# Block kernel: the Q/K stacks as blocks of 16 rows, with a second tile of tokens 768 to 2047

## The chip, the cores and the metric

The kernel runs on one core of a Trainium2 chip. A core has a matrix engine (TensorE, "PE" in the profile, with "PEld" for the loading of its weights), a vector engine (DVE), a scalar engine (ACT), GpSimd (POOL) and a sync engine (SP), from which this kernel issues its DMA transfers. The engines run their own instruction streams and meet at semaphores. Sixteen DMA engines carry the transfers. The metric is the device time of one execution in microseconds (us).

## What is computed

A transformer block for one sequence of 2048 tokens of width 640: attention with 32 heads of 20 dimensions, in which a token sees itself and the 255 tokens before it, and then a gated MLP with a mixing over the tokens. Cut to the part that the change touches:

```python
qkv = (layernorm(x) @ wqkv).reshape(B, S, 3, H, Dh).transpose(2, 0, 3, 1, 4)   # S 2048, H 32, Dh 20
q, k, v = qkv[0], qkv[1], qkv[2]
scores = einsum("bhqd,bhkd->bhqk", q, k) * Dh ** -0.5
mask = (idx[:, None] - idx[None, :] >= 0) & (idx[:, None] - idx[None, :] < 256)
p = softmax(where(mask, scores, -1e9), axis=-1)
h = x + einsum("bhqk,bhkd->bhqd", p, v).reshape(B, S, D) @ wo
h2 = h + gated_mlp(layernorm(h))
```

## The kernel before

**Stages.** By the profile's time: layer norm and V from 0 to 75 us, the projections to Q and K from 75 to 240 ("dense stage"), attention from about 240 to 468, the output projection to 550, then the MLP. The change touches the second and third stage.

**Splitting in three.** Q and K in float32 are each split in three bfloat16 parts (0 the largest). `split_qk(m, c)` does that for one of ten row tiles m (0 to 4 for the first 16 heads, 5 to 9 for the others; the 128 rows of a tile are eight of the 2 x 20 dimensions of Q and K, times 16 heads) and one of four column pieces c (512 tokens each), and stores all three parts with one DMA (L619) to `qk_d` in DRAM, 40 in all.

**Stacks.** Heads are worked in eight groups g of four. For a group, `load_stack(g)` reads Q and K back as stacks: a product of two numbers split in three is formed by laying six pairs of parts, (0,0), (0,1), (0,2), (1,0), (1,1), (2,0), one below another, so that a single matmul over 6 x 20 = 120 rows gives the sum of six products. `a` is 0 for Q and 1 for K. The stack of a group is in two tiles b, of 1024 tokens each (float32 words hold two bfloat16). Each load (L329) takes one part of one `a` and one b: 20 rows of 8 KB (four heads by 512 words) into partitions j, j+6, j+12 ... (`st[b][j:6 * DH:6, a]`), so 24 loads of 160 KB a group. Three sets of tiles are used in turn (`slot0`, `slot1`, and `xb`, which is the third set): group g takes set g mod 3.

**Items.** `max_item(g, qb, hh)` finds the row maxima of 128 queries of one head: four matmuls (L359), each of 32 queries against 288 keys, at four places of one bank, and a reduction on DVE (L369). For the first items it is one matmul of up to 384 keys (L363). `max_rows(g, b)` turns the maxima of eight blocks into three rows, stores them to `m_d` (L384) and loads them as rows 120 to 122 of the stack (L386). `score_item(u, hh)` then computes 128 keys against up to 384 queries over 123 rows, again in four strips (L412), and ACT takes the exponential (L415); `pv_item` multiplies with V and stores the output (L462).

**Cut strips.** Strips of keys or queries that cross token 1024 are in two tiles. `tokens()` (L332) yields the one or two pieces of a strip, and a matmul is issued for each piece, with its own weight load.

**Order.** PE, DVE, ACT and SP run in the order in which the program is written. The attention is a loop over steps s (L760), 16 to a group: in a step stand four max items of block s + 18 and four score items of block s in turns, and pieces of `pv_item(s - 2)`. `load_stack` is a generator; every `next` issues one DMA. In the dense stage three are drawn at a time; in the attention loop `1 + s % 2` in a step (24 in 16 steps). So loads for group s // 16 + 2 stand on SP's queue between the output stores and row loads of the steps. A DMA of SP also waits for the one issued eight before it.

Of the kernel before, what the change touches and what calls it, by code (L numbers as in the profile page):

```python
# [15 lines left out]
P = 128  # L16
S = 2048
# [17 lines left out]
def block_kernel(ctx, tc, x, xt, wqk, wv, wo, w_in, wsp, bsp, w_out, out):  # L35
# [15 lines left out]

    qk_d = dram.tile([2, 3, 2, 2 * DH, H // 2, S // 4], F32, name="qk_d")
    m_d = dram.tile([8, 2, 3, 32, 64], F32, name="m_d")
# [202 lines left out]
    with ExitStack() as ab:  # L256
# [8 lines left out]
        s0 = pool(low0, "slot0p")  # L265
        s0 = [s0.tile([P, 2 * S], F32R, name=f"slot0_{i}") for i in range(2)]
        xn = [h.rearrange("p (a k t) -> p a k t", a=2, k=KD) for h in (xa[:, :CH], xa[:, CH:], *xb)]
# [10 lines left out]
        add_slot(0, s0)  # L278
        add_slot(2, [h[:, :2 * S] for h in xb])
        mask = tmp2.tile([P, 384], BF16, name="mask")  # L280
# [35 lines left out]
        def load_stack(g):  # L316


            st = slot_w[g % 3]
            if g < 3:  # L320
                for h in st:
                    nc.gpsimd.memset(h[96:P, 1], ONES)
                    if g == 2:
                        yield
            for b in range(2):
                for j, parts in enumerate(((0, 0), (0, 1), (0, 2), (1, 0), (1, 1), (2, 0))):
                    for a in range(2):
                        src = qk_d[g // 4, parts[a], b, a * DH:(a + 1) * DH, g % 4 * 4:g % 4 * 4 + 4]
                        nc.sync.dma_start(st[b][j:6 * DH:6, a], src)  # L329
                        yield  # L330

        def tokens(st, rows, a, hh, t0, n):  # L332

            o = 0
            while o < n:
                c, t = divmod(t0 + o, S // 2)
                w = min(n - o, S // 2 - t)
                yield o, w, st[c][:rows, a, hh, t:t + w]
                o += w

        def one(st, rows, a, hh, t0, n):
            (_, _, x), = tokens(st, rows, a, hh, t0, n)
            return x

        def max_item(g, qb, hh, strips=True):

            st = slot_ap[g % 3]
            ps = s1_tile()
            lo = max(0, qb - 2) * P
            n = (qb + 1) * P - lo  # L350
            keep = mask[:, 384 - n:]
            if strips:
                skip = 32 if qb > 1 else 0
                if skip:
                    n, keep = 288, strip
                for j in range(4):
                    q0 = qb * P + 32 * j
                    for o, w, k in tokens(st, 120, 1, hh, lo + skip * j, n):
                        nc.tensor.matmul(ps[32 * j:32 * j + 32, o:o + w], one(st, 120, 0, hh, q0, 32), k,  # L359
                                         start=True, stop=True, tile_position=(0, 32 * j))  # L360
            else:
                for o, w, k in tokens(st, 120, 1, hh, lo, n):
                    nc.tensor.matmul(ps[:, o:o + w], one(st, 120, 0, hh, qb * P, P), k, start=True, stop=True)  # L363
            b, c = divmod(qb, 8)
            if c == 0 and hh == 0:
                m_cols[g, b] = tmp2.tile([P, 32], F32, tag="mcol", bufs=2, name=f"mcol{g}_{b}")
            junk = tmp2.tile([P, 384], BF16, tag="junk", bufs=2, name=f"junk{g}_{qb}_{hh}")
            c += hh * 8
            nc.vector.tensor_tensor_reduce(out=junk[:, :n], in0=ps[:, :n], in1=keep, scale=1.0,  # L369
                                           scalar=NEG, op0=OP.add, op1=OP.max, accum_out=m_cols[g, b][:, c:c + 1])  # L370

        def max_rows(g, b):

            ps = s1_tile()[:32, :P]
            nc.tensor.matmul(ps, m_cols.pop((g, b)), ident, start=True, stop=True)
# [10 lines left out]
            nc.sync.dma_start(slot_w[g % 3][b][120:123, 0], rows.rearrange("a (h r) c -> a h (r c)", h=4))  # L386
            yield
# [3 lines left out]
        def score_item(u, hh):  # L391
# [14 lines left out]
            for i in range(4):  # L406
                k0 = kb * P + 32 * i
                b, e = 32 * i, min(n, 32 * i + 288)
                if NU - NT < u and 4 * (u - NU + NT - 1) + hh < 6:
                    b, e = 0, n  # L410
                for o, w, q in tokens(st, 123, 0, hh, kb * P + b, e - b):
                    nc.tensor.matmul(ps[32 * i:32 * i + 32, b + o:b + o + w], one(st, 123, 1, hh, k0, 32), q,  # L412
                                     start=True, stop=True, tile_position=(0, 32 * i))
            if u <= NU - NT:
# [50 lines left out]
        if True:  # L465
# [137 lines left out]
            def split_qk(m, c, ps):  # L603
# [13 lines left out]
                T = S // 4  # L617
                base = qk_d[m // 5, 0, c // 2, m % 5 * 8, 0, c % 2 * 256:c % 2 * 256 + 256]
                nc.sync.dma_start(bass.AP(tensor=base.tensor, offset=base.offset,  # L619
                                          ap=[[T, P], [2 * 2 * DH * H // 2 * T, 3], [1, 256]]), sg.bitcast(F32))  # L620

# [84 lines left out]
            for n in range(24):  # L706
# [11 lines left out]
                if n >= 20:  # L718
                    for _ in range(3):
                        next(ld0, None)  # L720
            def dense_tail():
                split_wqk(8)
                split_wqk(9)
                for n, (m, c) in enumerate((m, c) for c in range(4) for m in (6, 7, 8, 9)):
# [3 lines left out]
                    if n == 7:  # L728
                        x01.close()
                        s1 = pool(x01, "slot1p", side="right")  # L730
                        add_slot(1, [s1.tile([P, 2 * S], F32R, name=f"slot1_{i}") for i in range(2)])
                    if n >= 7:
                        for _ in range(3):
                            next(ld1, None)

            dense = dense_tail()
            for n in range(12):
                next(dense, None)
                if n % 5 == 4:
                    for _ in range(3):  # L740
                        next(ld0, None)
            for u in range(LEAD):
# [8 lines left out]
                if u in (9, 17):  # L751
                    next(rows)
            assert next(dense, 0) == 0 and next(ld0, 0) == 0
            for _ in after[0]:
# [5 lines left out]
        for s in range(NU + 2):  # L760
            if s % NT == 0 and s < 6 * NT:
                ld = load_stack(s // NT + 2)
            for _ in range(1 + s % 2 if s >= NT else 2 * min(s, 1)):
                next(ld, None)
# [798 lines left out]
```

## Time and profile before

| what | value |
|---|---|
| median of 3 runs | 1105.15 us (1104.84 to 1106.06) |
| profiled execution, its own time | 1106.78 us |
| span of the profiled execution | 1105.1 us |
| PE busy over the span | 97%, 11059 matmuls recorded |
| DVE, ACT, POOL busy | 71%, 55%, 28% |
| granted TensorE clock | 1.00 |
| stack loads L329 | 192 of 160 KB, 160.5 to 412.3 us (the `xb` set from 245.6) |
| Q/K stores L619 | 40 of 384 KB, 93.4 to 244.7 us |

A row of the page or of a view names the source line, the engine, the operation, the output tile and the input tiles; then how often, how long, or what it waited for. In the busy table by stretches, the columns are the stretch, its length, busy us of PE, PEld, DVE, ACT and POOL with the number of instructions, the granted clock, the busy share of the 16 DMA engines, and GB/s. A row of a timeline is start, length, engine, line, operation, tiles, how many in a row, and in brackets the idle time before it with what ended it; "issue" means that nothing in the profile accounts for it. `slot,slot` as input means that a matmul's two operands are in two tiles.

### The profile page before, as it was taken

What the parts mean: (1) busy time and instruction counts of PE and PEld (TensorE: products, weight loads), DVE (VectorE), ACT (ScalarE), POOL (GpSimd) and SP (SyncE); (2) the same over time, 40 slices, a digit from 0 to 9 for tenths busy, and PEclk for the clock granted to TensorE, in tenths of its full rate; (3) what the DMA queues carried; (4) which work ended last, traced back from release to release, by engine and by line L of the source; (5) the groups of instructions that cost most, each with busy time, mean ns of one, the idle gap of its engine ahead of it and who ended that gap; (6) DMA issues with size and microseconds to landing.
All of it is one profiled execution on the core that took longest, in us unless ns stands there. A gap on an engine that the chain in (4) does not pass through costs nothing.

```text
span 1105.1 us, 28747 instructions
## 1 busy us (share of the span) xinstructions
PE 1075.2 (97%) x11059; PEld 968.4 (88%) x11059; DVE 781.0 (71%) x2157; ACT 604.7 (55%) x1258; POOL 314.0 (28%) x447
## 2 busy tenths in 40 slices
PE   8999999999999999999999999999999999999998
PEld 8998886658888787699999998999999899999998
DVE  6643445779999897575677668655556899987684
ACT  4443443249999899756766556443458433333331
POOL 4324446677766666721200012000001000000000
PEclk9999999999999999999999999999999999999999
DMA  7834657555565565689655342242441467684642
GB/s 252 296 115 118 175 172 262 169 181 171 190 188 189 178 192 151 183 263 296 252 184 174 131 142 77 66 133 97 127 148 51 173 223 254 229 276 137 195 141 96
DMA packets 92281, 194.73 MB, mean 176 GB/s; under 512 B 11952, under 2 KB 46272, under 8 KB 88256
## 3 DMA queue, kind: packets, MB, share of 16 engines
q1 hardware_dynamic: 92144, 192.90, 53.4%
q8 instruction: 87, 1.43, 0.6%
q14 instruction: 50, 0.41, 0.1%
HBM read 127.90 MB, written 64.95 MB: 175 GB/s over the span
## 4 chain that ended last, share of the span: by engine, by line
PE 79%; DMA 6%; ACT 4%; DVE 4%; issue 4%; POOL 2%; SPq 1%; DVEq 0%; POOLq 0%; ACTq 0%
PE g L1181 23%; PE pv L440 6%; PE bank L359 5%; PE bank L412 5%; PE zb L1066 4%; PE qk L592 4%; PE qk L594 4%; PE qk L593 4%; PE out_x L1345 3%; PE zx L1006 2%; PE out_v L1345 2%; PE zv L1006 2%; DMA h_d<-xh 1%; PE zy L1006 1%; PE zw L1006 1%
## 5 line engine op out<-in xcount | busy, mean ns | idle before, releaser
L415 ACT ACTIVATE pt<-bank 128x384 f32<-128x384 f32 (+1 forms) x452 | 180.2, 483 | 17.2 <-PE bank L412 10.8
L1181 PE MATMUL g<-zl,aw 128*128 128x432 f32 x768 | 169.1, 357 | 1.5 <-ACT zl L828 1.0
L369 DVE CUSTOM_DVE_ANT_0 junk<-bank,strip 128x288 bf16<-128x288 f32 x392 | 156.1, 452 | 12.3 <-PE bank L359 10.1
L828 ACT ACTIVATE aw<-fx 128x512 fp32r<-128x512 f32 (+2 forms) x152 | 86.2, 587 | 127.6 <-DVE fx L822 57.9
L1181 PEld LDWEIGHTS g<-zl,aw 128*128 128x128 f32 x768 | 144.0, 188 | 8.1 <-ACT zl L828 1.4
L440 PE MATMUL pv<-pt,v_sb 128*32 128x192 f32 (+3 forms) x1984 | 135.2, 322 | 4.6 <-POOL pt L419 2.4
L822 DVE TENSOR_TENSOR aw<-fx,aw 128x512 fp32r<-128x512 f32 (+2 forms) x152 | 95.8, 638 | 60.1 <-ACT aw L828 59.8
L1181 PE MATMUL g<-ze,aw 128*128 128x432 f32 x576 | 132.6, 359 | 2.3 <-DVE row L822 2.3
L1181 PEld LDWEIGHTS g<-ze,aw 128*128 128x128 f32 x576 | 107.1, 188 | 9.0 <-DVE row L822 3.7
L419 POOL TENSOR_SCALAR_AFFINE_SELECT pt<-pt 128x512 f32<-128x512 f32 x128 | 83.5, 653 | 61.2 <-ACT pt L415 59.0
L412 PE MATMUL bank<-slot 123*32 123x288 bf16 (+8 forms) x1296 | 95.7, 273 | 2.0 <-issue 1.3
L359 PE MATMUL bank<-slot 120*32 120x288 bf16 (+6 forms) x1248 | 93.5, 275 | 0.9 <-DVE mcol L369 0.8
L440 PEld LDWEIGHTS pv<-pt,v_sb 128*32 128x32 f32 x1984 | 65.5, 110 | 11.9 <-POOL pt L419 6.2
L422 POOL TENSOR_SCALAR_AFFINE_SELECT pt<-pt 128x512 f32<-128x512 f32 x112 | 71.2, 635 | 0.0
L412 PEld LDWEIGHTS <-slot 123*32 123x32 bf16 x1728 | 58.8, 96 | 13.0 <-issue 3.6
L359 PEld LDWEIGHTS <-slot 120*32 120x32 bf16 x1408 | 52.1, 95 | 15.2 <-issue 7.2
L369 DVE CUSTOM_DVE_ANT_0 junk<-bank,mask 128x384 bf16<-128x384 f32 (+2 forms) x120 | 51.2, 444 | 17.0 <-PE bank L363 15.7
L822 DVE TENSOR_TENSOR row<-g,row 128x432 f32<-128x432 f32 x80 | 48.3, 603 | 21.0 <-PE g L1181 20.6
L616 POOL TENSOR_TENSOR sg<-rest,sg 128x512 bf16<-128x512 f32 x40 | 46.7, 1167 | 56.3 <-ACT sg L615 45.6
L606 DVE TENSOR_TENSOR rest<-qk,std 128x512 f32<-128x512 f32 x40 | 27.6, 690 | 44.9 <-PE qk L594 44.9
L608 ACT ACTIVATE sg<-rest 128x512 bf16<-128x512 f32 x40 | 25.2, 631 | 54.3 <-DVE rest L606 54.3
L118 PE MATMUL wo_ps<-xb,xb 128*128 128x320 f32 x260 | 52.4, 311 | 1.5 <-DVE mvc L1460 1.5
(263 smaller groups left out, 2538.4 us busy)
## 6 DMA issues: line engine op xcount, KB each, us to landing
slot<-qk_d SPq DMA_DIRECT2D x144, 160.0 KB
fx<-wsp_in SPq DMA_DIRECT2D x32, 512.0 KB
qk_d<-sg SPq DMA_DIRECT2D x40, 384.0 KB
o_d<-ot SPq DMA_DIRECT2D x64, 128.0 KB
xb<-qk_d SPq DMA_DIRECT2D x48, 160.0 KB
fx<-hn_d SPq DMA_DIRECT2D x24, 320.0 KB
z_d<-row SPq DMA_DIRECT2D x16, 432.0 KB
g_d<-row SPq DMA_DIRECT2D x16, 432.0 KB
```

The costliest lines, as they stand in the source:

```text
L359: nc.tensor.matmul(ps[32 * j:32 * j + 32, o:o + w], one(st, 120, 0, hh, q0, 32), k, start=True, stop=True, tile_position=(0, 32 * j))
L369: nc.vector.tensor_tensor_reduce(out=junk[:, :n], in0=ps[:, :n], in1=keep, scale=1.0, scalar=NEG, op0=OP.add, op1=OP.max, accum_out=m_cols ...
L412: nc.tensor.matmul(ps[32 * i:32 * i + 32, b + o:b + o + w], one(st, 123, 1, hh, k0, 32), q, start=True, stop=True, tile_position=(0, 32 * i))
L415: nc.scalar.activation(pt[:, hh, :n], ps[:, :n], AF.Exp, scale=SCALE)
L419: nc.gpsimd.affine_select(out=pt[:, :, :P], in_=pt[:, :, :P], pattern=[[0, 4], [1, P]], base=0, channel_multiplier=-1, compare_op=OP.is_ge ...
L422: nc.gpsimd.affine_select(out=pt[:, :, 256:], in_=pt[:, :, 256:], pattern=[[0, 4], [-1, P]], base=-1, channel_multiplier=1, compare_op=OP. ...
L440: nc.tensor.matmul(ps[32 * hh:32 * hh + 32, a - 512 * c:b - 512 * c], v_sb[:, kb, v0:v0 + 32], pt[:, hh, a - kb * P:b - kb * P], start=fir ...
L822: (eng or nc.vector).tensor_tensor(out=out, in0=a, in1=b, op=op)
L828: nc.scalar.activation(out, a, AF.Copy)
L1006: nc.tensor.matmul(ps, a[x], b[:, y], start=start and m + x + y == 0, stop=stop and m == n - 1 and x == 1, skip_group_check=True)
L1181: nc.tensor.matmul(ps, w[m][:, x, k], zc[k][m][:, y], start=start and k + x + y == 0, stop=stop and k == 3 and x == 1, skip_group_check=True)
L1345: nc.tensor.matmul(o[b][:, :HD], l[:, x, k * P:(k + 1) * P], r[k][:, y], start=start and k + x + y == 0, stop=stop and k == 2 and x == 1, ...
```

## The change

- The second tile of a stack holds tokens 768 to 2047 (640 words a row instead of 512, the first tile is unchanged). So no strip crosses a tile's end, `tokens()` is gone, and each strip is one matmul. Tokens 768 to 1023 are stored, loaded and kept twice, the row maxima of these too (a second row load for b = 0).
- In DRAM there are four tensors in place of one: `qk_d[b]` with the first 16 of a part's 20 dimensions, and `qr_d[b]` with the last four, which are stored once for each of the six pairs in which the part stands. The rows of a stack are ordered accordingly: pair j has partitions 16j to 16j + 15, and the last four dimensions of all six pairs are in partitions 96 to 119.
- A group's loads are, for each b, twelve of 16 rows into neighbouring partitions and two of 24 rows: 28 in place of 24. Four are drawn at a time in the dense stage, and in the attention `1 + (s % 4 > 0)` in a step.
- A row tile's store is one DMA or, for c = 1, two; of m = 4 and m = 9, which hold the last four dimensions, six or, for c = 1, twelve. That makes 100 in place of 40. The columns of the weights are reordered on the host to this end.

TensorE, in the second group, the first item whose keys cross token 1024 (block 8). `slot1_0` and `slot1_1` are the two tiles of its stack, `bank2` is the place of the result. Before, four strips in two pieces each:

```order
L359 LDWEIGHTS slot1_1_1978
L359 MATMUL bank2_121<-slot1_0_1977,slot1_1_1978 32x256
L359 LDWEIGHTS slot1_1_1978
L359 MATMUL bank2_121<-slot1_1_1978 32x32
L359 LDWEIGHTS slot1_1_1978
L359 MATMUL bank2_121<-slot1_0_1977,slot1_1_1978 32x224
L359 LDWEIGHTS slot1_1_1978
L359 MATMUL bank2_121<-slot1_1_1978 32x64
```

Now, two of the four strips, each whole and out of the second tile:

```order
L356 LDWEIGHTS slot1_1_2024
L356 MATMUL bank2_124<-slot1_1_2024 32x288
L356 LDWEIGHTS slot1_1_2024
L356 MATMUL bank2_124<-slot1_1_2024 32x288
```

Of 16 instructions for this item 8 are left; the order of items around it is the same.

SP, near the end of the dense stage, where the first loads of group 0 (`slot0_0`) stand between stores (`sg4_1` is the split of row tile 4, piece 1). Before:

```order
L619 DMA qk_d_64<-sg4_1_1520 128x3x256
L586 DMA std4_3_1551<-rstd_d_69 128x512
L556 DMA wqraw8_1553<-wqk_in 128x640
L619 DMA qk_d_64<-sg5_1_1548 128x3x256
L329 DMA slot0_0_102<-qk_d_64 20x2048 x3
```

Now, from the seventh of the twelve stores of `sg4_1`:

```order
L638 DMA qr_d1_67<-sg4_1_1532 64x3x128
L638 DMA qr_d1_67<-sg4_1_1532 64x2x128
L638 DMA qr_d1_67<-sg4_1_1532 64x128
L638 DMA qr_d1_67<-sg4_1_1532 64x3x128
L638 DMA qr_d1_67<-sg4_1_1532 64x2x128
L638 DMA qr_d1_67<-sg4_1_1532 64x128
L590 DMA std4_3_1574<-rstd_d_72 128x512
L560 DMA wqraw8_1576<-wqk_in 128x640
L630 DMA qk_d0_64<-sg5_1_1571 128x3x256
L630 DMA qk_d1_65<-sg5_1_1571 128x3x128
L332 DMA slot0_0_105<-qk_d0_64 16x2048 x4
```

One store has become twelve, the next one two, and loads come four at a time, of 16 rows.

```diff
-    qk_d = dram.tile([2, 3, 2, 2 * DH, H // 2, S // 4], F32, name="qk_d")
+    WORDS = (S // 4, S // 4 + P)
+    qk_d = [dram.tile([2, 2, 3, 16, H // 2, n], F32, name=f"qk_d{b}") for b, n in enumerate(WORDS)]
+    qr_d = [dram.tile([2, 2, 6, DH - 16, H // 2, n], F32, name=f"qr_d{b}") for b, n in enumerate(WORDS)]
+    PAIRS = ((1, 0), (0, 1), (0, 0), (0, 2), (2, 0), (1, 1))
...
             for b in range(2):
-                for j, parts in enumerate(((0, 0), (0, 1), (0, 2), (1, 0), (1, 1), (2, 0))):
+                for j, parts in enumerate(PAIRS):
                     for a in range(2):
-                        src = qk_d[g // 4, parts[a], b, a * DH:(a + 1) * DH, g % 4 * 4:g % 4 * 4 + 4]
-                        nc.sync.dma_start(st[b][j:6 * DH:6, a], src)
+                        nc.sync.dma_start(st[b][16 * j:16 * j + 16, a], qk_d[b][q, a, parts[a], :, heads])
                         yield
+                for a in range(2):
+                    nc.sync.dma_start(st[b][96:6 * DH, a], qr_d[b][q, a, :, :, heads].rearrange("j d h t -> (j d) h t"))
+                    yield
...
-                    for o, w, k in tokens(st, 120, 1, hh, lo + skip * j, n):
-                        nc.tensor.matmul(ps[32 * j:32 * j + 32, o:o + w], one(st, 120, 0, hh, q0, 32), k,
-                                         start=True, stop=True, tile_position=(0, 32 * j))
+                    nc.tensor.matmul(ps[32 * j:32 * j + 32, :n], one(st, half_b, 120, 0, hh, q0, 32),
+                                     one(st, half_b, 120, 1, hh, lo + skip * j, n),
+                                     start=True, stop=True, tile_position=(0, 32 * j))
...
-            nc.sync.dma_start(slot_w[g % 3][b][120:123, 0], rows.rearrange("a (h r) c -> a h (r c)", h=4))
+            rows, st = rows.rearrange("a (h r) c -> a h (r c)", h=4), slot_w[g % 3]
+            if b == 0:
+                nc.sync.dma_start(st[0][120:123, 0], rows)
+                nc.sync.dma_start(st[1][120:123, 0, :, :P], rows[:, :, 6 * P // 2:])
+            else:
+                nc.sync.dma_start(st[1][120:123, 0, :, P:], rows)
...
-                nc.sync.dma_start(bass.AP(tensor=base.tensor, offset=base.offset,
-                                          ap=[[T, P], [2 * 2 * DH * H // 2 * T, 3], [1, 256]]), sg.bitcast(F32))
+                for b in range(2):
...
+                    if m % 5 < 4:
...
+                        nc.sync.dma_start(bass.AP(tensor=base.tensor, offset=base.offset,
+                                                  ap=[[W, P], [16 * n * W, 3], [1, t1 - t0]]), part)
+                        continue
+                    for a in range(2):
+                        for p in range(3):
+                            js = [j for j, x in enumerate(PAIRS) if x[a] == p]
...
+                            nc.sync.dma_start(bass.AP(tensor=base.tensor, offset=base.offset,
+                                                      ap=[[W, 64], [4 * n * W * step, len(js)], [1, t1 - t0]]),
+                                              part[64 * a:64 * a + 64, p:p + 1].to_broadcast([64, len(js), t1 - t0]))
...
-            for _ in range(1 + s % 2 if s >= NT else 2 * min(s, 1)):
+            for _ in range(1 + (s % 4 > 0) if s >= NT else 2 * min(s, 1)):
```

More of the change, by code (lines that the diff above doesn't have):

```diff
@@ L265, in block_kernel @@
         s0 = pool(low0, "slot0p")
-        s0 = [s0.tile([P, 2 * S], F32R, name=f"slot0_{i}") for i in range(2)]
+        s0 = [s0.tile([P, 8 * n], F32R, name=f"slot0_{i}") for i, n in enumerate(WORDS)]
         xn = [h.rearrange("p (a k t) -> p a k t", a=2, k=KD) for h in (xa[:, :CH], xa[:, CH:], *xb)]
@@ L278, in block_kernel @@
         add_slot(0, s0)
-        add_slot(2, [h[:, :2 * S] for h in xb])
+        add_slot(2, [h[:, :8 * n] for h, n in zip(xb, WORDS)])
         mask = tmp2.tile([P, 384], BF16, name="mask")
@@ L357, in max_item @@
                     q0 = qb * P + 32 * j
-                    for o, w, k in tokens(st, 120, 1, hh, lo + skip * j, n):
-                        nc.tensor.matmul(ps[32 * j:32 * j + 32, o:o + w], one(st, 120, 0, hh, q0, 32), k,
-                                         start=True, stop=True, tile_position=(0, 32 * j))
-            else:
-                for o, w, k in tokens(st, 120, 1, hh, lo, n):
-                    nc.tensor.matmul(ps[:, o:o + w], one(st, 120, 0, hh, qb * P, P), k, start=True, stop=True)
+                    nc.tensor.matmul(ps[32 * j:32 * j + 32, :n], one(st, half_b, 120, 0, hh, q0, 32),
+                                     one(st, half_b, 120, 1, hh, lo + skip * j, n),
+                                     start=True, stop=True, tile_position=(0, 32 * j))
+            else:
+                nc.tensor.matmul(ps[:, :n], one(st, half_b, 120, 0, hh, qb * P, P), one(st, half_b, 120, 1, hh, lo, n),
+                                 start=True, stop=True)
             b, c = divmod(qb, 8)
@@ L410, in score_item @@
                     b, e = 0, n
-                for o, w, q in tokens(st, 123, 0, hh, kb * P + b, e - b):
-                    nc.tensor.matmul(ps[32 * i:32 * i + 32, b + o:b + o + w], one(st, 123, 1, hh, k0, 32), q,
-                                     start=True, stop=True, tile_position=(0, 32 * i))
+                c = int(kb > 5)
+                nc.tensor.matmul(ps[32 * i:32 * i + 32, b:e], one(st, c, 123, 1, hh, k0, 32),
+                                 one(st, c, 123, 0, hh, kb * P + b, e - b),
+                                 start=True, stop=True, tile_position=(0, 32 * i))
             if u <= NU - NT:
@@ L718, in block_kernel @@
                 if n >= 20:
-                    for _ in range(3):
+                    for _ in range(4):
                         next(ld0, None)
@@ L730, in dense_tail @@
                         s1 = pool(x01, "slot1p", side="right")
-                        add_slot(1, [s1.tile([P, 2 * S], F32R, name=f"slot1_{i}") for i in range(2)])
+                        add_slot(1, [s1.tile([P, 8 * n], F32R, name=f"slot1_{i}") for i, n in enumerate(WORDS)])
                     if n >= 7:
-                        for _ in range(3):
+                        for _ in range(4):
                             next(ld1, None)
@@ L739, in block_kernel @@
                 if n % 5 == 4:
-                    for _ in range(3):
+                    for _ in range(4):
                         next(ld0, None)
@@ L752, in block_kernel @@
                     next(rows)
-            assert next(dense, 0) == 0 and next(ld0, 0) == 0
+            assert next(dense, 0) == 0 and next(ld0, 0) == 0 and next(ld1, 0) == 0
             for _ in after[0]:
@@ L1544 @@
     w = np.asarray(A_wqkv).reshape(D, 3, H, DH)
-    wqk = w[:, :2].reshape(D, 2, 2, H // 2, DH).transpose(2, 1, 4, 0, 3).reshape(2 * D // P, 8, KD, P, H // 2)
+    wqk = w[:, :2].reshape(D, 2, 2, H // 2, DH).transpose(2, 1, 4, 0, 3)
+    wqk = np.concatenate([wqk[:, a, d] for d in (slice(0, 16), slice(16, DH)) for a in range(2)], axis=1)
+    wqk = wqk.reshape(2 * D // P, 8, KD, P, H // 2)
     wqk = wqk.transpose(0, 3, 2, 1, 4).reshape(2 * D // P, P, KD, P)
```

26 lines of the change are left out of this document (14 added, 12 removed).

## The prediction

> **What bounds the kernel now.** The page's first part comes first, then the busy table by stretches of the attention, then the cut matmuls, and last the sync queue that loads the stacks.
>
> ```profile
> PE 1075.2 (97%) x11059; PEld 968.4 (88%) x11059; DVE 781.0 (71%) x2157; ACT 604.7 (55%) x1258; POOL 314.0 (28%) x447
> 240.00:268.00 28.00, 26.17 (x779) 21.54 (x782) 26.21 (x134) 25.60 (x65) 22.34 (x35) 1.00 0.52 162
> ...
> 408.00:436.00 28.00, 26.41 (x788) 22.12 (x784) 25.06 (x129) 24.66 (x65) 18.41 (x32) 1.00 0.54 161
> sum 196.00, PE 186.82 PEld 157.56 DVE 182.75 ACT 178.94 POOL 137.36; mean PE 26.69 PEld 22.51 DVE 26.11 ACT 25.56 POOL 19.62
> ```
>
> TensorE is busy 97% of the span, at full clock in each stretch. In the 196 us of attention it is idle for 196.00 - 186.82 = 9.2 us, and VectorE and ScalarE follow it closely (182.75 and 178.94). So a shorter attention needs less TensorE work or less of these 9.2 us, as long as the stacks keep coming. The cut matmuls are those that name two tiles:
>
> ```profile
> L359 PE MATMUL bank<-slot,slot x160: 179/227/275, 251.5 to 425.8; 120*32 120x256 bf16 x20, 120*32 120x224 bf16 x20, 120*32 120x192 bf16 x20, 120*32 120x160 bf16 x20
> L359 PE MATMUL bank<-xb,xb x64: 179/228/275, 279.1 to 368.0; 120*32 120x256 bf16 x8, 120*32 120x224 bf16 x8, 120*32 120x192 bf16 x8, 120*32 120x160 bf16 x8
> L412 PE MATMUL bank<-slot,slot x160: 177/224/272, 251.7 to 426.0; 123*32 123x128 bf16 x20, 123*32 123x96 bf16 x20, 123*32 123x64 bf16 x20, 123*32 123x32 bf16 x20
> L412 PE MATMUL bank<-xb,xb x64: 177/224/270, 306.8 to 396.7; 123*32 123x128 bf16 x8, 123*32 123x96 bf16 x8, 123*32 123x64 bf16 x8, 123*32 123x32 bf16 x8
> ...
> L412 PE MATMUL pair<-slot,slot x32: 177/224/270, 448.4 to 450.6; 123*32 123x128 bf16 x4, 123*32 123x96 bf16 x4, 123*32 123x64 bf16 x4, 123*32 123x32 bf16 x4
> L363 PE MATMUL bank<-slot,slot x8: 231/258/285, 206.0 to 212.8; 120*128 120x256 bf16 x4, 120*128 120x128 bf16 x4
> ```
>
> They are 224 + 256 + 8 = 488, each with a partner. What a cut step costs shows in TensorE's order of time:
>
> ```profile
> 303.30 0.31 PE L359 MATMUL bank<-slot 120*32 120x288 bf16 x4
> ...
> 304.95 0.31 PE L359 MATMUL bank<-slot 120*32 120x288 bf16 x4
> ...
> 306.62 0.27 PE L359 MATMUL bank<-slot,slot 120*32 120x256 bf16 x4
> ...
> 308.49 0.21 PE L359 MATMUL bank<-slot,slot 120*32 120x96 bf16 x3
> ...
> 310.69 0.20 PE L359 MATMUL bank<-slot,slot 120*32 120x64 bf16 x2 [0.98 <-issue]
> ```
>
> A plain step takes 1.65 us (303.30 to 304.95, and 1.67 to 306.62), the first cut step 1.87 (with two small matmuls of the row maxima in it). The second has a stall of 0.98 us of which no engine is the cause ("issue").
>
> **What the change takes away.** Two cut steps in each of seven groups, at 0.1 us of added issue each (half of the 0.2 excess; the other half I leave to the two extra matmuls): 14 x 0.1 = 1.4 us. The stalls are worth at most the 9.2 us of idle. I take 6 of these, since the seen stall stands in a cut step and the rest has other causes: 7.4 us in all, bounds 1.4 and 10.6. This gain is real only if the stacks come in time.
>
> **What it adds to the transfers.** How fast a load goes depends on the partitions it reaches:
>
> ```profile
> 1.70 2.33 SPq L629 DMA_DIRECT2D wvraw<-wv_in  x5
> 9.00:12.00 3.00, 2.60 (x15) 2.18 (x16) 3.00 (x6) 2.61 (x8) 2.71 (x3) 1.00 1.05 378
> 245.60 5.99 SPq L329 DMA_DIRECT2D xb<-qk_d  x8
> 246.50:252.00 5.50, 5.50 (x183) 4.78 (x172) 5.36 (x29) 5.46 (x15) 4.24 (x7) 1.00 0.60 194
> 467.57 2.03 SPq L178 DMA_DIRECT2D m<-o_d  x4
> 468.90:470.10 1.20, 1.20 (x10) 1.20 (x10) 1.12 (x2) 0.52 (x2) 0.00 (x0) 1.00 0.90 281
> 470.10:471.20 1.10, 1.10 (x9) 1.10 (x8) 0.97 (x2) 0.00 (x0) 0.00 (x0) 1.00 1.00 251
> ```
>
> The last two columns are the busy share of the 16 DMA engines and GB/s. Weights into 128 partitions go at 378. The stack loads of now, 20 rows six partitions apart, go at 194 with a share of 0.60: about ten engines of sixteen carry them, and each of these moves 20 GB/s. The loads of line 178, into 32 neighbouring partitions, fill the engines (1.00) and yet move only 251, so there the engines wait for something on the receiving side. The new loads go into 16 neighbouring partitions, and both heads' halves `a` of one part into the same 16. No row shows such a load. It could go at 251 or more, if only the engines count; if what holds the 32 is shared out by neighbours, at half of 251, **125 GB/s**; less than half is unlikely, since a block of 32 is two of 16. I take 125, since the row nearest in shape is the one that shows a limit at full engines, and 188 (24/32 of 251) for the blocks of 24.
>
> In 1000-byte KB a group then takes: tile 0, 12 x 131/125 + 2 x 197/188 = 14.7 us; tile 1, whose rows are 1.25 times as long, 18.4 us; together 33.1. The eight output stores of a group, 131 KB each at 378, add 2.8: **36 us a group**. The groups now follow one another at 29.3 us (from the load row at 245.60 to the step at 421.50, quoted below, there are six), so the load becomes the bound.
>
> [...]
>
> ```profile
> 160.00:174.00 14.00, 14.00 (x62) 11.23 (x61) 6.06 (x9) 6.30 (x10) 7.02 (x6) 1.00 0.84 280
> 170.61 0.38 SPq L619 DMA_DIRECT2D qk_d<-sg  x1
> 178.42 0.22 PE L363 MATMUL bank<-slot 120*128 120x128 bf16 x1 [0.15 <-DMA slot<-qk_d]
> ...
> 421.50 0.34 PE L359 MATMUL bank<-slot,slot 120*32 120x256 bf16 x3
> ```
>
> **The first group.** Its first matmul at 178.42 already waits 0.15 us for its load, so nothing covers a later one. Tile 0 is 1966 KB before and after: 10.1 us at 194, now 14.7, so 4.6 later. Two of the doubled stores (of m=4, the one at 170.61 and the one of the m=4 item before it) add 393 KB each, 2.8 us at 280; of the 14 us here 16% are free, 2.2 us. That makes 5.2 to 7.4; I take **6 us** late. TensorE's order is fixed, so all behind it slips too.
>
> **The chain.** Loads of the third group start at 245.60, now 251.6. Six groups follow one another, 6 x 36 = 216: the last tile 1 is there at 467.6. The step that needs it first starts now at 421.50 (its cut matmul names both tiles). That is +46.1. What is saved behind this point is at most the idle of the last stretch, 28.00 - 26.41 = 1.6; I take 1.5. What is saved ahead of it only makes TensorE wait longer. Sum: 1106.8 (profiled execution; span 1105.1) + 46.1 - 1.5 = 1151.4. That execution lies 1.6 above the median of the runs, so **1150 us**. With six groups between 251.6 and 421.5, 28.3 us each, less 2.8 for stores, the loads are hidden if they take 25.5 us: the point is 125 x 33.1/25.5 = 162 GB/s for blocks of 16.
>
> **The other edits.** The stores rise from 40 to 100:
>
> ```profile
> L619 SPq DMA_DIRECT2D qk_d<-sg x40: 359/366/422, 93.4 to 244.7; - x40
> L329 SPq DMA_DIRECT2D slot<-qk_d x144: 694/703/1202, 160.5 to 412.3; - x144
> L386 SPq DMA_DIRECT2D slot<-m_d x12: 262/269/364, 217.8 to 442.8; - x12
> SPq L386 <- DMA m_d<-m: 15.9, 13, 2.8
> ```
>
> 60 x 0.37 = 22 us of SP time more between 93 and 245, beside TensorE's work; behind them on the queue stand the loads of the first group, and if one store's source is late, they are too (in the 6 us). Eight more row loads for the maxima, 0.27 each, are 0.3 us a group and hidden. The larger memset and the changed column order of the weights issue no more instructions; nothing.
>
> **Rivals.** *Faster:* blocks of 16 use all engines and the limit of line 178 doesn't fall further, so they go at 162 or more. Then loads stay hidden and the 7.4 us are gained: 1106.8 - 7.4 - 1.6 = 1098 (1094.6 to 1103.8 by the bounds). For it speaks the share of 0.60, which leaves six engines unused, and that loads are issued eight in a row (the x8 row), so that several blocks may be filled together; against it, that line 178 has four blocks in flight and full engines and reaches 251 only. [...]
>
> *Sync queue:* rates hold, but SP becomes the bound. A load costs SP 0.70 whatever its rows, so four more a group and one more row load are 4 x 0.70 + 0.27 = 3.1 us; before, 24 x 0.70 = 16.9 us and the waits of the other instructions filled most of 28. If those waits don't shrink, 6 x 3.1 - 1.5 = +17: 1122. Against: waits for results shrink when SP is late.
>
> *No change:* the rate lies close to 162 and a late tile takes the gain back, 1103 to 1107. That the change does not do what it says is excluded: the instruction order has no matmul of two tiles left.
>
> **How the numbers follow.** Forecast .62; faster .26; sync queue .06; no change .06. The forecast's own range: half of the higher 281 gives 141 GB/s, 32.1 us a group and 1127; at 125 with two waits of 2.8 us a group in which no load can be issued (the row of L386), 41.6 us a group and 1184. The range reaches down into the faster case, 1096, and up to 1186. About 0.2% is what a measurement of this kernel tells from no change; by it .26 faster, .06 same, .68 slower.
>
> **What would show it.** Right: from 250 on the busy table shows DMA at about 125 to 140 GB/s with a share near 1.00, first matmuls of a group wait for "DMA slot", groups 36 us apart, TensorE idle above 40 us between 240 and 480. The 6 us: the first matmul of line 363 starts near 184. Wrong: GB/s at 162 or more, no waits for "DMA slot", steps of 1.65 us throughout; then the faster rival holds, and it is the rate for 16 partitions that I had mis-sized. Issue stalls that stay though no step is cut would show the 6 of 7.4 us wrong.

## The result and the profile after

The changed kernel takes 1189.32 us (median of 6 runs, 1186.64 to 1195.01) against 1104.99 of before (6 runs): ratio 1.0774, 95% interval 1.0745 to 1.0803. The profiled execution took 1190.28 us, its span is 1188.5. The forecast was slower, 1150 us, with a range up to 1186; the direction came true, the time lies beyond the range.

The first part of the page and then the busy table by stretches, of the changed kernel (columns as before):

```profile
PE 1096.5 (92%) x10571; PEld 977.9 (82%) x10571; DVE 785.2 (66%) x2157; ACT 609.0 (51%) x1258; POOL 315.0 (27%) x447
184.00:212.00 28.00, 20.20 (x77) 12.78 (x78) 10.23 (x39) 5.67 (x9) 9.91 (x9) 0.72 1.03 186
280.00:320.00 40.00, 34.21 (x870) 26.78 (x862) 31.21 (x154) 30.31 (x79) 23.06 (x41) 0.91 0.90 149
...
440.00:480.00 40.00, 28.72 (x716) 23.47 (x712) 25.52 (x129) 24.90 (x65) 18.36 (x32) 0.91 0.90 148
```

The 488 matmuls are gone (11059 to 10571), and yet TensorE has fallen from 97% to 92% of a longer span. In the attention the DMA engines are 90% busy and move 149 GB/s. The same stretch of the kernel before:

```profile
280.00:320.00 40.00, 38.46 (x1191) 33.00 (x1188) 37.87 (x191) 36.93 (x96) 28.11 (x50) 1.00 0.60 189
```

Per busy engine that is 149 / (16 x 0.90) = 10.3 GB/s in place of 189 / (16 x 0.60) = 19.7: a busy engine moves about half as much.

Where the time went is read best from the sync queue: the first load of the third group and of the eighth, for before and for the changed kernel (start, length, engine, line, operation, tiles, how many in a row):

```profile
245.60 0.74 SPq L329 DMA_DIRECT2D xb<-qk_d  x1
386.48 1.51 SPq L329 DMA_DIRECT2D slot<-qk_d  x2
```

```profile
277.04 1.89 SPq L332 DMA_DIRECT2D xb<-qk_d  x2
463.83 1.95 SPq L332 DMA_DIRECT2D slot<-qk_d  x3
```

Up to the third group the change loses 277.0 - 245.6 = **31.4 us**. From there to the eighth, five groups, it goes at (463.8 - 277.0) / 5 = **37.4 us a group** in place of 28.2, so five times 9.2 = 46 us more; the last group and the end add the remaining 6 of the 83.4 by which the span grew. These two numbers, the *start* (of the third group's loads) and the *pace* (us a group), are taken from the profile of each experiment below.

The 31.4 us arise at few places. The timeline of TensorE, with the idle time ahead of an instruction in brackets:

```profile
183.95 0.76 PE L596 MATMUL qk<-xa,wqh 128*128 128x512 f32 x1 [7.38 <-DVE rest L610]
194.65 0.27 PE L360 MATMUL bank<-slot 120*128 120x128 bf16 x1 [7.80 <-DMA slot<-qr_d]
261.20 0.43 PE L356 MATMUL bank<-slot 120*32 120x288 bf16 x4 [3.03 <-DVE mcol L367]
270.85 0.43 PE L415 MATMUL bank<-slot 123*32 123x288 bf16 x4 [7.78 <-ACT pt L419]
```

Together 26.0 us; where the other 5.4 arise was not placed. Only the second is the wait that the prediction had for the first group. The first ends when VectorE has waited for a small load of `std`, which stands on the sync queue among stores and stack loads:

```profile
183.12 1.29 DVE L610 TENSOR_TENSOR rest<-qk,std 128x512 f32<-128x512 f32 x2 [3.50 <-DMA std<-rstd_d]
```

What else delays the first, and what is behind the last, shows in the table of waits of ScalarE between 140 and 280 us (who waited for what: total, times, longest):

```profile
ACT sg L612 <- DMA qk_d<-sg: 26.4, 7, 5.2
...
ACT sg L612 <- DMA qr_d<-sg: 15.3, 5, 3.6
```

Before, that table between 140 and 250 us has no row with a DMA in it. ScalarE may write a new split (`sg`) only when the store of an older one has landed, and the stores now land late. On the sync queue a repeated store stands for up to 9.6 us:

```profile
153.74 9.62 SPq L638 DMA_DIRECT2D qr_d<-sg  x12
163.46 0.53 SPq L590 DMA_DIRECT2D std<-rstd_d  x1
...
L638 SPq DMA_DIRECT2D qr_d<-sg x60: 468/584/1109, 146.3 to 275.4; - x60
```

### The profile page after: what moved, and what is told of

It reads as the page before. It is cut to its first block, busy times and chain, and to the rows that moved or that the text cites. A ratio compares the mean times of both kernels' runs of the same rounds, so it can differ in the third digit from the quotient of the medians.

```text
span 1188.5 us, 27934 instructions
## 1 busy us (share of the span) xinstructions
PE 1096.5 (92%) x10571; PEld 977.9 (82%) x10571; DVE 785.2 (66%) x2157; ACT 609.0 (51%) x1258; POOL 315.0 (27%) x447
## 4 chain that ended last, share of the span: by engine, by line
PE 65%; DMA 13%; issue 6%; DVE 6%; ACT 5%; POOL 2%; SPq 2%; POOLq 0%; DVEq 0%; ACTq 0%
PE g L1201 21%; PE pv L444 4%; PE bank L356 4%; PE bank L415 3%; PE out_x L1365 3%; PE qk L596 3%; PE qk L598 3%; PE qk L597 3%; PE zb L1086 3%; DMA slot<-qk_d 2%; PE zx L1026 2%; DMA xh<-x_in 2%; PE out_v L1365 2%; PE zv L1026 2%; DMA m_d<-m 1%
## 5 line engine op out<-in xcount | busy, mean ns | idle before, releaser
L419 ACT ACTIVATE pt<-bank 128x384 f32<-128x384 f32 (+1 forms) x452 | 183.9, 479 | 65.7 <-PE bank L415 53.6
L367 DVE CUSTOM_DVE_ANT_0 junk<-bank,strip 128x288 bf16<-128x288 f32 x392 | 159.8, 452 | 64.2 <-PE bank L356 61.0
L444 PE MATMUL pv<-pt,v_sb 128*32 128x192 f32 (+3 forms) x1984 | 146.9, 335 | 20.6 <-issue 18.4
L415 PE MATMUL bank<-slot 123*32 123x288 bf16 (+6 forms) x1296 | 106.6, 298 | 14.3 <-ACT pt L419 8.2
L356 PE MATMUL bank<-slot 120*32 120x288 bf16 (+2 forms) x1248 | 104.3, 303 | 10.2 <-issue 6.5
L444 PEld LDWEIGHTS pv<-pt,v_sb 128*32 128x32 f32 x1984 | 72.3, 114 | 30.8 <-issue 21.5
L612 ACT ACTIVATE sg<-rest 128x512 bf16<-128x512 f32 x40 | 25.2, 631 | 82.8 <-DVE rest L610 38.4
```

What stands on the lines that cost most here:

```text
L356: nc.tensor.matmul(ps[32 * j:32 * j + 32, :n], one(st, half_b, 120, 0, hh, q0, 32), one(st, half_b, 120, 1, hh, lo + skip * j, n), start=T ...
L415: nc.tensor.matmul(ps[32 * i:32 * i + 32, b:e], one(st, c, 123, 1, hh, k0, 32), one(st, c, 123, 0, hh, kb * P + b, e - b), start=True, sto ...
L419: nc.scalar.activation(pt[:, hh, :n], ps[:, :n], AF.Exp, scale=SCALE)
L444: nc.tensor.matmul(ps[32 * hh:32 * hh + 32, a - 512 * c:b - 512 * c], v_sb[:, kb, v0:v0 + 32], pt[:, hh, a - kb * P:b - kb * P], start=fir ...
```

## The experiments

Thirteen kernels ran. The table has their medians, the ratio to before with its 95% interval, and start and pace as defined above (from one profiled execution each). That execution lies up to 5.6 us from the median: e2, e3, e9 and e11 were profiled in their fastest, e1 and e4 in their slowest. And e10 has a pace 1.1 above that of before at a time that is the same within 0.3%. So a difference of one us in start or pace says nothing by itself. Each ratio is to the kernel before as measured beside that run (1101.34 to 1104.99), so runs of different rows are compared by their ratios.

| run | us | ratio | start | pace |
|---|---|---|---|---|
| before | 1104.99 | | 245.6 | 28.2 |
| changed | 1189.32 | 1.0774 (1.0745 to 1.0803) | 277.0 | 37.4 |
| e1 16 rows spread | 1131.12 | 1.0248 (1.0204 to 1.0291) | 264.9 | 30.8 |
| e2 before, 20 neighbours | 1132.28 | 1.0255 (1.0231 to 1.0278) | 251.9 | 31.1 |
| e3 strips alone | 1115.71 | 1.0102 (1.0077 to 1.0127) | 247.4 | 30.1 |
| e4 other order of loads | 1158.96 | 1.0493 (1.0473 to 1.0514) | 273.1 | 32.7 |
| e5 two large stores | 1182.90 | 1.0734 (1.0693 to 1.0776) | 271.5 | 36.7 |
| e6 both, e1 and e5 | 1120.10 | 1.0167 (1.0126 to 1.0208) | 254.1 | 30.1 |
| e7 before, sixty stores more | 1124.42 | 1.0201 (1.0168 to 1.0234) | 269.4 | 27.9 |
| e8 one load for several pairs | 1377.23 | 1.2493 (1.2456 to 1.2531) | 315.7 | 61.6 |
| e9 strips, loads early | 1121.56 | 1.0170 (1.0149 to 1.0191) | 246.9 | 30.9 |
| e10 before, loads early | 1104.76 | 1.0016 (1.0000 to 1.0032) | 245.2 | 29.3 |
| e11 strips, rows one step later | 1106.76 | 1.0014 (0.9996 to 1.0033) | 246.5 | 27.9 |
| e12 before, rows one step later | 1105.28 | 1.0005 (0.9984 to 1.0025) | 246.2 | 27.9 |
| e13 strips, rows two steps later | 1104.45 | 0.9993 (0.9974 to 1.0012) | 247.8 | 27.1 |

### Neighbouring partitions: e1, e2 and e4

e1, on the changed kernel:

```diff
-                        nc.sync.dma_start(st[b][16 * j:16 * j + 16, a], qk_d[b][q, a, parts[a], :, heads])
+                        nc.sync.dma_start(st[b][j:96:6, a], qk_d[b][q, a, parts[a], :, heads])
```

> The changed kernel, but the loads of 16 rows go into partitions j, j+6 ... j+90 instead of 16 neighbours; bytes, number of loads and stores are the same. Theory N (neighbouring partitions make each row slow, and all that queues behind them): the groups follow at about 29 us again, which takes back some 52 us of the 84, and part of what the dense stage lost: 1105 to 1137 us. Theory V (12.5% more bytes and four more loads a group): 1180 to 1190. Theory S (the sixty small stores set the loss in the dense stage, whatever the loads do): the attention is as N says, but its start stays some 30 us late, 1132 to 1140.

Measured: 1131.12, 58 us less than the changed kernel, by nothing but the partitions that the same bytes go to. Pace 30.8; of the start, 12 of the 31.4 us are taken back. The time lies in N's bounds; V, in the form that bytes and number alone explain it, falls, though the pace stays 2.6 above that of before. S is not refuted: its lower bound is 0.9 us away, and the start is still 19.3 us late. e5 to e7 take it up. The busy table of e1 in its attention:

```profile
268.00:296.00 28.00, 26.89 (x768) 22.34 (x764) 26.43 (x135) 26.18 (x68) 19.43 (x34) 1.00 0.70 191
```

A busy engine moves 191 / (16 x 0.70) = 17 GB/s, against 10.3. The traced packets say the same: between 280 and 460 us a row of 8 KB took a median of 0.31 us before, 0.68 in the changed kernel and 0.46 in e1.

e2, on the kernel before:

```diff
-                        nc.sync.dma_start(st[b][j:6 * DH:6, a], src)
+                        nc.sync.dma_start(st[b][DH * j:DH * j + DH, a], src)
```

> The kernel before, with its loads of 20 rows put into 20 neighbouring partitions instead of every sixth; nothing else. N: an 8 KB row takes about 0.66 us instead of 0.31, as in the changed kernel, so 24 loads of two rows on each of ten engines are some 33 us a group and with the output stores 36 to 40: 1140 to 1170 us. V and S: nothing changes, 1103 to 1107.

Measured: 1132.28, 28 us more than before: 8 us below N's bounds and far from V's. A row of 8 KB took a median of 0.51 us there and not the 0.66 that N assumed. Neighbours cost in the old kernel too, with no byte more. The sync queue's rows show the other side of it:

```profile
L329 SPq DMA_DIRECT2D slot<-qk_d x144: 272/330/1553, 160.5 to 438.9; - x144
```

The same load holds the sync queue for a median of 330 ns with neighbours and 703 with every sixth partition: issuing is cheaper, moving dearer (0.51 us a row in place of 0.31).

e4, on the changed kernel:

```diff
-                for j, parts in enumerate(PAIRS):
-                    for a in range(2):
-                        nc.sync.dma_start(st[b][16 * j:16 * j + 16, a], qk_d[b][q, a, parts[a], :, heads])
-                        yield
+                for a in range(2):
+                    for j in (0, 4, 1, 5, 2, 3):
+                        nc.sync.dma_start(st[b][16 * j:16 * j + 16, a], qk_d[b][q, a, PAIRS[j][a], :, heads])
+                        yield
```

> The changed kernel with its 16-row loads drawn in another order, so that loads in a row go to blocks far apart (pairs 0, 4, 1, 5, 2, 3, first for Q, then for K) and not twice to the same 16 partitions. If the DMA engines run apart and what is in flight together counts: 20 us or more faster than the changed kernel, 1150 to 1170. If the engines go through the loads in step, each load by itself: 1184 to 1195.

Measured: 1158.96, 30 us less than the changed kernel, by order alone: what is in flight together counts, as the first expectation has it. The changed kernel sends two loads one behind the other into the same 16 partitions, and e4 doesn't.

```profile
280.00:320.00 40.00, 36.97 (x989) 30.47 (x985) 34.86 (x176) 33.81 (x87) 25.00 (x43) 0.96 0.84 182
```

### The stores: e5, e6 and e7

e7 adds the sixty small stores to the kernel before, where nobody reads them (its own 40 stay):

```diff
+                if m % 5 < 4:
+                    return
+                for b in range(2):
...
+                    for a in range(2):
+                        for p in range(3):
...
+                            nc.sync.dma_start(bass.AP(tensor=base.tensor, offset=base.offset,
+                                                      ap=[[W, 64], [4 * n * W * step, len(js)], [1, t1 - t0]]),
+                                              part[64 * a:64 * a + 64, p:p + 1].to_broadcast([64, len(js), t1 - t0]))
```

> The kernel before, with the sixty small stores of the change added to its own (nobody reads them), all else unchanged. I: the loads behind them are late though they are as quick as before: 1115 to 1130. E: 1105 to 1112, since the stores hurt only where slow loads fill the engines.

Measured: 1124.42, 23 us more than its own before (1101.34), within the bounds of I. First loads of the third and the eighth group:

```profile
269.42 1.61 SPq L332 DMA_DIRECT2D xb<-qk_d  x2
...
408.95 1.54 SPq L332 DMA_DIRECT2D slot<-qk_d  x2
```

The start is 23.8 us late, and the pace is that of before. So the stores alone are enough for three quarters of the 31.4 us, with loads as quick as ever. ScalarE's waits for stores are there too, 30.2 us between 140 and 275.

e5 replaces, in the changed kernel, the six or twelve DMAs of a repeated store:

```diff
                     for a in range(2):
-                        for p in range(3):
-                            js = [j for j, x in enumerate(PAIRS) if x[a] == p]
-                            base = qr_d[b][m // 5, a, js[0], 0, 0, o:o + t1 - t0]
...
+                        base = qr_d[b][m // 5, a, 0, 0, 0, o:o + t1 - t0]
+                        nc.sync.dma_start(bass.AP(tensor=base.tensor, offset=base.offset,
+                                                  ap=[[W, P], [P * W, 3], [1, t1 - t0]]), part)
```

> The changed kernel, but where a row tile is stored repeated (m = 4 and 9), two DMAs of 128 rows by three parts take the place of the six of 64 rows, so 20 in place of 60 with the same bytes; what they write there is in the wrong places, so the sum of products is not the right one. Theory I (the issue time of the small stores on the sync queue, 60 x 0.58 us, and the loads queued behind them set the lateness of the dense stage): some 20 us faster than the changed kernel, 1164 to 1174 us. Theory E (the DMA engines are full there, and stores and loads take the same time however they are issued): 1183 to 1193.

Measured: 1182.90, at E's lower bound. I falls here: the ratios to before of this kernel and of the changed one, 1.0734 and 1.0774, have intervals that overlap, so no gain can be told. With slow loads it matters little how the stores are issued.

e6 is e5 with the line of e1:

> As the last, and also the 16-row loads into every sixth partition (which alone gave 1131). It writes the repeated rows in the wrong places too. I: the start of the attention comes forward by up to 19 us, 1112 to 1120. E: with the loads quick, the engines have room and the stores cost little either way: 1126 to 1133.

Measured: 1120.10, at the edge of I, and by the ratios about 9 us less than e1 (1.0167 and 1.0248; their intervals just touch). With quick loads the number of stores seems to matter (start 254.1 against 264.9, and ScalarE waits 5.9 us for stores between 140 and 270 in place of 20.7). Slow loads and many stores thus hide one another: each alone delays the start, by 25.9 (e5, few stores, neighbours) and 19.3 us (e1, many stores, spread), both together by 31.4, and neither by 8.5 (e6). They don't add up, so no share can be given to each.

### The strips alone: e3, e9, e10, e11, e12 and e13

e3 keeps the tile of tokens 768 to 2047 and the whole strips, with loads and stores as before:

```diff
-                        src = qk_d[g // 4, parts[a], b, a * DH:(a + 1) * DH, g % 4 * 4:g % 4 * 4 + 4]
-                        nc.sync.dma_start(st[b][j:6 * DH:6, a], src)
+                        nc.sync.dma_start(st[b][j:6 * DH:6, a], qk_d[b][q, parts[a], a * DH:(a + 1) * DH, heads])
...
-            nc.sync.dma_start(slot_w[g % 3][b][120:123, 0], rows.rearrange("a (h r) c -> a h (r c)", h=4))
+            rows, st = rows.rearrange("a (h r) c -> a h (r c)", h=4), slot_w[g % 3]
+            if b == 0:
+                nc.sync.dma_start(st[0][120:123, 0], rows)
+                nc.sync.dma_start(st[1][120:123, 0, :, :P], rows[:, :, 6 * P // 2:])
+            else:
+                nc.sync.dma_start(st[1][120:123, 0, :, P:], rows)
```

> The second tile with tokens 768 to 2047 and whole strips, but 24 loads of 20 rows into every sixth partition and one store per piece as before (two at c = 1): the part of the change that removes matmuls, alone. The prediction's gain: 7.4 us faster, 1095 to 1102 us. V: the longer rows of tile 1 are 12.5% more bytes on ten engines, loads come late or delay code loading: 1105 to 1115.

Measured: 1115.71, 11.6 us more than before. The gain of 7.4 that the prediction gave the strips isn't there, and the time is 0.7 us above V's bounds. A matmul of its attention and the sync queue ahead of it:

```profile
369.74 0.43 PE L352 MATMUL bank<-xb 120*32 120x288 bf16 x4 [2.99 <-DMA xb<-qk_d]
```

```profile
363.43 1.50 SPq L331 DMA_DIRECT2D xb<-qk_d  x2
367.83 0.74 SPq L385 DMA_DIRECT2D slot<-m_d  x1
```

The last two loads of the tile were issued at 363.4 to 364.9, and TensorE waits for them until 369.74.

e9 draws the loads of e3 earlier, e10 those of before in the same way:

```diff
-            for _ in range(1 + s % 2 if s >= NT else 2 * min(s, 1)):
+            for _ in range(2 * min(s, 1)):
```

> Strips whole and 24 loads of 20 rows into every sixth partition, as in the run of the strips alone (1115.7), but two loads are issued in each attention step until a group's 24 are out, in place of one and two in turn. Theory Q (there the last loads of the second tile stood too far back on the sync queue, behind stores and row loads that wait for results; the three matmul waits for loads go, and the strips' gain shows): 1094 to 1103 us. Theory T (the sync queue's or the loads' total time a group is the limit, wherever they stand): 1108 to 1118.

> The kernel before with two loads a step in the same way, nothing else. In its profile no matmul of the attention waits for a load, so Q gives no change, 1102 to 1106. If loads that come faster delay the code loading more, the issue stalls grow: 1106 to 1112.

Measured: 1121.56 and 1104.76. Q falls: earlier loads make e3 slower, not faster, and 3.6 us beyond T's bounds too. The kernel before doesn't change beyond what can be told. What waits in e9 is no longer a load but the row maxima (TensorE's idle time, and the sync queue's waits from 260 to 420 us):

```profile
372.78 0.31 PE L411 MATMUL bank<-slot 123*32 123x288 bf16 x4 [2.50 <-DMA slot<-m_d]
```

```profile
SPq L385 <- DMA m_d<-m: 16.6, 5, 4.0
...
SPq L382 <- DMA m_d<-m: 6.2, 5, 2.2
```

The sync queue stands still for up to 4.0 us before a row load, until the store to `m_d` just ahead of it has landed, and all behind it waits. This speaks for the queue's whole time being short, so that whatever stands last on it is late; e11 tests it.

e11 (on e3) and e12 (on before) move the row load one step away from that store, e13 (on e3) two steps:

```diff
-                if hh == 3 and u1 % 8 == 1 and s <= NU - LEAD + 1:
-                    next(rows)
+                if hh == 3 and u1 % 8 == 2 and s <= NU - LEAD + 2:
+                    next(rows, None)
```

> Strips whole and 24 loads of 20 rows (1115.7 alone), but the row loads of the maxima are issued one step later, so that one or two stack loads stand between the store to m_d and the load that waits for it. Theory W (the sync queue is the bound there, and its waits for m_d, some 2.4 us a group or more, are part of its time): 1102 to 1110 us, and the matmuls' waits for slot and xb loads shrink. Theory L (the waits come from the loads' own length, 12.5% more bytes): 1113 to 1119.

> The kernel before with the row loads one step later in the same way. In its attention no matmul waits for a load, so the sync queue's time is hidden: 1101 to 1106 by both theories. If the sync queue's lag also sets when code is loaded, fewer issue stalls: 1095 to 1100.

> As the last run of the strips (1106.8 beside 1104.8 of before), with the row loads of the maxima two steps later than at first instead of one. W: the 9.3 us in which the sync queue still waits for m_d shrink and the gain of the strips shows against before, 1097 to 1103. If the rows now come too late for the scores that need them: 1108 to 1125.

Measured: 1106.76, 1105.28 and 1104.45. W holds for e11, 9 us less than e3 by a later row load alone; its matmuls of the attention wait for no stack load any more, and 1.7 us for rows. e12 doesn't move, as expected, since nothing in its attention waits for the queue. e13 gains no more that could be told from e11, against the expectation: whole strips are even with before (0.9974 to 1.0012), with a gain of at most 3 us in that interval. The sync queue's waits for `m_d` did shrink, to 0.4 us between 240 and 480. None of the versions beats the kernel before.

### One load for several pairs: e8

```diff
+    LOADS = ((0, 2, 3, 0), (1, 1, 2, 1), (0, 0, 2, 1), (1, 4, 2, 0), (0, 5, 1, 2), (1, 0, 1, 0), (1, 3, 1, 2))
...
+                for a, j0, nj, part in LOADS:
...
+                    src = bass.AP(tensor=src.tensor, offset=src.offset, ap=[[0, nj], *src.ap])
+                    nc.sync.dma_start(st[b][DH * j0:DH * (j0 + nj), a], src)
```

In the dense stage it also draws two loads an item in place of three.

> The kernel before, with strips cut as before, but one load writes a part to all neighbouring pairs of the stack that hold it: 14 loads a group in place of 24, of 20, 40 and 60 rows into as many neighbouring partitions, bytes the same. If what the sync queue spends on loads holds the groups at 28.2 us: 1096 to 1103. If blocks of 20 and 40 neighbours are slow enough to make loads late: 1108 to 1130.

Measured: 1377.23, far beyond both. Its busy table:

```profile
400.00:440.00 40.00, 11.10 (x194) 7.88 (x194) 7.33 (x36) 6.67 (x19) 4.68 (x9) 0.58 0.23 77
```

From the first `xb` load to 740 us TensorE waits 134.4 us for row loads of the maxima and 41.2 for stack loads. They are late while the DMA engines are idle for three quarters of the time. A busy engine moves 77 / (16 x 0.23) = 21 GB/s, no less than before, so it isn't the partitions: too few engines are at work, 3.7 of 16 on average (0.23 x 16). What keeps the others idle was not shown: four of a tile's seven loads now repeat their rows 3 or 2 times, and no run varied that by itself.

## Why the prediction was right in direction and wrong in size and in the wait

**Half right: the loads into 16 neighbours slow the attention, but not by the wait that was forecast.** e1, e2 and e4 show the partitions as the cause from three sides, and the group's time was put at 36 us and came to 37.4. Its sign was to be that the first matmuls of a group wait for "DMA slot". Between 280 and 500 us no matmul of the changed kernel waits for a stack load, and the weight loads do for 3.7 us. TensorE stops where neither an engine nor a transfer is named, for 38.4 us:

```profile
PE pv L444 <- issue: 16.1, 7, 3.9
PE bank L356 <- issue: 11.3, 5, 4.2
PE bank L415 <- issue: 11.0, 6, 2.9
```

```profile
PEld L356 <- DMA xb<-qk_d: 3.5, 1, 3.5
PEld L356 <- DMA slot<-qk_d: 0.2, 1, 0.2
```

From the third group's first load to the last output matmul (`pv`), these stops of matmuls come to 40.7 us in the changed kernel, 39.7 in e5, 24.0 in e4 and 21.9 in e2, all with neighbours; without neighbours they are 6.6 in the kernel before, 4.8 in e1, 8.6 in e6 and 6.0 in e7. That stretch lasts 273.9 us in place of 222.6. Of the 51.3 more, 34.1 are these stops, and 12.4 are busy time of TensorE, whose granted clock there is 0.94 in place of 1.00, though it has some 540 matmuls fewer. Whether the stacks would have been late had TensorE not stopped stays open: with the DMA engines 90 to 96% busy from 280 to 480 us, the loads have little room to be quicker. In e2, with the engines 64% busy over that stretch and hardly a wait for a load (0.2 us, at a weight load), it is the stops that lengthen the attention (15.3 of 19.4 us).

**Luck in the rate.** The 125 GB/s is half of 251, and the row with 251 has four blocks of 32 in flight together; it isn't the rate of one block. By the forecast's sizes the loads of a group are 4424 KB. Over a group that is 118 GB/s in the changed kernel and 135 in e4 (pace 32.7), which has the same blocks in another order. So the rate hangs on an order that the prediction named and did not price. The 125 to 140 GB/s in its list of signs don't follow from its own sum either: 4424 KB of loads and 1049 of output stores in 36 us are 152, and 148 to 157 were seen.

**Wrong, the step that failed: the first group, "I take 6 us late".** It was 31.4. The step had one wait, the one before 178.42; that wait is there (7.80 us, the row at 194.65). Missing were the stops behind it: a split waits until an older store has landed, and in "the other edits" the sixty stores were given 22 us of sync-queue time "beside TensorE's work". A store took 0.58 us and not 0.37 (35 us in all), and e7 shows that these stores alone, with quick loads, make the start 23.8 us late. What was to hide them was TensorE's dense work, and that work waits for the very buffers that the stores hold. The stores are not the only cause: in e5, with 20 large ones in place of the sixty, slow loads alone still make the start 25.9 us late. That slow loads hold up the stores, and through them the dense stage, is the other thing that the step left out.

**A term too small: the chain.** It gave six groups 6.7 us each more, 40 us. The pace shows 9.2 a group: 1.4 because a group took 37.4, and 1.1 because the groups of before follow at 28.2 and not at 29.3; the span from the third group's first load to the eighth group's first use of its second tile is longer than six paces. The miss of 39 us against 1189 is thus 25 in the start and about 13 in the chain.

**Wrong, though hidden: the gain of 7.4 us by whole strips.** e3 has it alone and is 11.6 slower, and with the sync queue relieved (e13) it is even. Part of the term is there: matmuls' issue stops, of which the prediction took 6 us, fall from 6.6 us before to 0.9 in e11 and 2.2 in e13, and from the start to the last `pv` matmul the two take 218.7 and 218.2 us against 222.6 (221.9 in e12). But the start comes 0.9 and 2.2 us later, and the rest of the kernel differs between executions by about as much as is gained, so that nothing shows in the time. What e3 pays was forecast at 0.3 us a group and hidden: a group's row loads hold the queue for 0.27 + 0.74 + 0.74 us there in place of twice 0.27, 1.2 us more, and the queue is what is short. Of the forecast's sum only 1.5 us rested on this gain, but the rival "faster", 1098 at a chance of .26, rested on it wholly.

**The rivals.** No run shows the premise of the faster rival, blocks of 16 at 162 GB/s or more: over a group the loads went at 118 in the changed kernel and at 135 in e4. The sync queue rival had the mechanism that holds e3 back (it gave 1122 for 28 loads a group; e3 has 24 and took 1115.7). In the changed kernel itself its price is not there: a load of 16 neighbours holds the queue 0.42 us and not 0.70, as that rival had assumed.

```profile
L332 SPq DMA_DIRECT2D slot<-qk_d x144: 302/418/1550, 165.6 to 492.5; - x144
```

## What to carry to other kernels

Look at a load's destination before its size: the same bytes in the same number of loads took 58 us more of this kernel when each load went into a narrow block of neighbours, and 30 of them came back when loads in flight together were sent to blocks far apart. Count the stores of a stage by what waits for their buffers, not by the engine they run beside: sixty more of them alone made the start 23.8 us late in e7. When loads go into narrow blocks, look for stops of TensorE with no wait named, and not only for late data: here they were 40.7 us in place of 6.6. And a queue that stands still for a result (up to 4.0 us in e9) holds up all that is behind it: moving one waiting instruction by a step was worth 9 us in e11, and drawing the loads earlier was worth less than nothing in e9 (ratio 1.0170 against 1.0102 of e3).

## What the runs showed of the hardware

- TensorE's granted clock was lower in stretches in which it stood idle: 0.72 between 184 and 212 us of the changed kernel (busy 20.20 of 28) and 0.971 over its span, against 1.00 before; in e8, with TensorE busy 11.10 of 40 us, it was 0.58. It doesn't follow the busy time closely: in the changed kernel it was 0.91 from 280 to 320 us (busy 34.21 of 40) and 0.96 from 320 to 360 (31.55).
- In the changed kernel, with the DMA engines 90 to 96% busy from 280 to 480 us, TensorE stops, for up to 4.2 us at a matmul and 4.6 at a weight load, at places where no engine and no transfer is named ("issue"). In the table of waits between 240 and 560 us such stops are TensorE's largest rows (a matmul's stop and that of its weight load are often the same one; the 8.1 lies ahead of 280 us):

```profile
PEld L415 <- issue: 28.7, 17, 8.1
PEld pv L444 <- issue: 21.5, 10, 4.2
PEld L356 <- issue: 18.7, 30, 4.1
PE pv L444 <- issue: 18.4, 8, 3.9
```

What ends them is in the trace of the DMA packets. The page of the changed kernel lists two queues of the kind "instruction" beside that of the loads:

```profile
q1 hardware_dynamic: 102512, 202.39, 63.8%
q8 instruction: 83, 1.36, 0.6%
q14 instruction: 51, 0.42, 0.2%
```

From 277 to 551 us, all 19 issue stops of matmuls in the changed kernel end 1.2 to 2.0 us after a packet of q8 (16 KB) has landed; a moment picked at random lies so far behind such a packet with a chance of 0.13. In e5, e4 and e2 the same holds for all 17, 13 and 10 stops. That q8 brings TensorE's instructions fits its 83 packets for 21142 matmuls and weight loads, where the kernel before has 87 for 22118: 255 and 254 to a packet. So these look like instructions that come late. Why the loads into neighbours make them late was not taken apart. The mean share of the engines doesn't tell it: from the third group's first load to the last `pv` matmul e2 has 21.9 us of such stops at a share of 0.64, and e1 4.8 at 0.66.
